# Keys in blocks of 64 throughout an attention stage: values on four tiles of the array

## The chip, the core and the metric

The kernel runs on one core of a Trainium2 chip. The core has a matrix engine (TensorE, PE in the profile, with PEld for its weight loads), a vector engine (VectorE, DVE), a scalar engine (ScalarE, ACT) and GpSimd (POOL); SyncE (SP) issues most of the transfers. Every engine works through its own instructions in order and waits for others by semaphores. PSUM, where TensorE writes its products, has eight banks of 512 fp32 columns on 128 partitions; all other on-chip data lie in SBUF. The metric is the device time of one execution in microseconds, as a median over runs.

## The reference

Attention with 8 batches, 8 heads, 576 positions and 64 channels a head. A query sees itself and the 127 positions before it, with a penalty that grows with the distance, by a slope for each head. The result goes, token by token, through a mixture of experts: a gate picks one of 8 experts for each of the 4608 tokens.

```python
rel = pos[:, None] - pos[None, :]
slopes = 2.0 ** (-8.0 * (np.arange(H, dtype=np.float32) + 1) / H)
bias = slopes[:, None, None] * (-np.abs(rel).astype(np.float32))[None, :, :]
mask = (rel >= 0) & (rel < window)                      # window = 128
scores = np.where(mask, scale * q @ k.T + bias, -1e9)
attn = np.exp(scores - max); attn = attn / (sum(attn) + 1e-9); x = attn @ v
logits = x @ w_gate; e = argmax(logits)                 # per token
y = gate_w * (relu(x @ w1[e]) @ w2[e])
```

## The kernel before

It has two stages. The first is attention, with the gate and the routing woven in; the second runs the experts over the rows that routing has sorted into DRAM. The change touches the first stage alone.

**Units.** Attention is cut into 32 units, one for each batch and pair of heads (`NU`, L497); a pair's 2 x 64 channels fill 128 partitions. The maximum isn't subtracted: exp(score) is multiplied by a table of exp(-slope x distance), which is zero outside the window. A unit goes through these steps:

- `scores` (L584): keys on the partitions, queries along the columns. Key blocks of 128 are taken as two halves of 64 keys (`HBLK`), each against the at most 192 queries that can see them, one product for each half and head, on a 64 x 64 quarter of the array. They fill four PSUM banks `sp`, 512 columns each; the corners that no product writes were cleared once (L520). ScalarE takes the exponential of each bank (L599).
- `factors` (L601): VectorE multiplies by the table, in two halves of the columns, 1024 elements each (L606, L611).
- `merge` (L613): VectorE adds two stretches of probabilities that belong to the same queries (L617), so that their sums need one product.
- `values` (L621): 128 keys by 64 channels as weights, the probabilities streamed, both heads beside each other on the columns of the array; queries 0 to 255 in one bank, 256 to 575 in another. ScalarE copies both to `xT` (L642).
- `totals` (L644): the sums of the probabilities for every query, by a product with a column of ones that selects a row for the pair of heads; all four pairs of a batch collect in one bank `sm`. At the batch's end `sm` is copied to `sT` (L669, L670).

**Tasks.** What follows attention for a batch is cut into tasks (`tasks_of`, L747): two for the gate's logits (`logits_t`), two or three `gate` tasks (transposes of logits and sums, L694 and L697, reciprocals, products with them, the minimum L713, then ScalarE's exponentials L716, and the pick of the expert), `row` (transposes of `xT` back to tokens and VectorE's scaling by 1/sum, L739), `place` (the rank of each token), and sends of rows by indirect transfers from POOL (L192).

**Order.** It is written out by hand (`manual_schedule`). In the main loop (L798 to L832) iteration u issues the loads for unit u + 4, scores of u, the first half of its factors, one task, the second half and the merge, then values and totals of unit u - 1, then two to four more tasks. Tasks start at u = 9. `last_tasks` (L768) handles the last batch, with the first layer of an early group of tokens put between.

**Buffers.** PSUM: four `sp` banks, one `sm`, and three `m` banks that values, logits, gate, place and row share in turn: each allocation waits until what stood in the bank three allocations before has been read. The load pool `ld` has five buffers each for queries and keys and two for values.

**Transfers.** SP issues queries, keys and values in the loop's order, with eight clearings of the routed rows between (`clear_rows`, units 1 to 10) and the first expert's weights at unit 16.

Of the kernel before, what the change touches and what calls it, by code (L numbers as in the profile page):

```python
# [8 lines left out]
F32 = mybir.dt.float32  # L9
I32 = mybir.dt.int32  # L10
# [5 lines left out]
P = 128  # L16
# [5 lines left out]
def kernel(  # L22
# [474 lines left out]
    NU = NB * HP  # L497

    BLK = [(j, 2 * P * j, P * j, 2 * P) for j in range(KT - 1)]
    BLK += [(KT - 1, 2 * P * (KT - 1), P * (KT - 1), P + HALF), (KT, 2 * P * KT - HALF, P * KT, HALF)]  # L500

    HBLK = []
    for j, c, q0, n in BLK[:-1]:
        HBLK += [(P * j, 0, c, q0, min(n, P + HALF)), (P * j + HALF, 1, c + HALF, q0 + HALF, min(n - HALF, P + HALF))]
    HBLK.append((P * KT, 1, BLK[-1][1], P * KT, HALF))
    W = 2 * P * KT
    SEG = ((0, 2 * P), (2 * P, S - 2 * P))
    QB = HP + 1
    with tc.tile_pool(name="tab", bufs=1) as tab, \
# [7 lines left out]

        sp_banks = [ps_s.tile([P, W // 2], F32, name=f"sp{i}") for i in range(4)]
        for sp in sp_banks:
            nc.vector.memset(sp[:], 0.0)  # L520

        rels = ex.tile([P, 2, W], F32, name="probs")
        rel_i, rel = rels.bitcast(I32)[:, 0, : 2 * P], rels[:, 1, : 2 * P]
        nc.gpsimd.iota(rel_i, pattern=[[1, 2 * P]], base=0, channel_multiplier=-1)
        nc.gpsimd.tensor_copy(rel, rel_i)

        fac2 = tab.tile([P, H, W // 2], F32, name="fac2")
        fac = fac2[:, :, : 2 * P]

        def distances(hp):  # L530
            pair = fac[:, 2 * hp : 2 * hp + 2, :]
            for i in range(2):
                nc.vector.tensor_scalar_mul(pair[:, i, :], rel, 2.0 ** (-8.0 * (2 * hp + i + 1) / H))
            nc.gpsimd.affine_select(
                pair, pair, compare_op=ALU.is_ge, fill=MASKED,
                base=0, pattern=[[0, 2], [1, 2 * P]], channel_multiplier=-1,
            )
            nc.gpsimd.affine_select(
                pair, pair, compare_op=ALU.is_gt, fill=MASKED,
                base=P, pattern=[[0, 2], [-1, 2 * P]], channel_multiplier=1,  # L540
            )

        def table(hp):
            heads = slice(2 * hp, 2 * hp + 2)
            nc.scalar.activation(fac[:, heads, :], fac[:, heads, :], AF.Exp, scale=-1.0)
            nc.vector.tensor_copy(fac2[:, heads, 2 * P : 3 * P + HALF], fac[:, heads, : P + HALF])
            nc.vector.tensor_copy(fac2[HALF:, heads, 3 * P + HALF :], fac[HALF:, heads, HALF:P])

        for hp in range(HP):
            distances(hp)  # L550
# [3 lines left out]
        nc.vector.memset(fac2[:HALF, :, 3 * P + HALF :], 0.0)  # L554
# [3 lines left out]
        for hp in range(HP):  # L558
            nc.vector.memset(one_c[:, hp, hp : hp + 1], 1.0)
# [8 lines left out]
        q_sb, k_sb, v_sb, xT, lT, sT = {}, {}, {}, {}, {}, {}  # L568
        early = {}
        probs, exps, mgs, sums = {}, {}, {}, {}  # L570
# [8 lines left out]
        def load_v(b):  # L579
            v_sb[b] = ld.tile([P, KT + 1, Dm], F32, name="v_sb", bufs=2)  # L580
            nc.sync.dma_start(v_sb[b][:, :KT, :], v[b * S : b * S + KT * P, :].rearrange("(t p) d -> p t d", p=P))
            nc.sync.dma_start(v_sb[b][:, KT, :], v[(b + 1) * S - P : (b + 1) * S, :])

        def scores(u):  # L584
            b, hp = divmod(u, HP)
            probs[u] = ex.tile([P, 2, W], F32, name="probs")
            sps = sp_banks[:2], sp_banks[2:]
            for k0, part, c, q0, n in HBLK:
                s, c = divmod(c, W // 2)
                for par in range(2):  # L590
                    half = slice(par * HALF, (par + 1) * HALF)
                    nc.tensor.matmul(  # L592
                        sps[s][par][part * HALF : (part + 1) * HALF, c : c + n], lhsT=k_sb[u][half, k0 : k0 + HALF],
                        rhs=q_sb[u][half, q0 : q0 + n], start=True, stop=True,
                    )
            exps[u] = [ex.tile([P, 2, W // 2], F32, name="e") for _ in range(2)]
            for s in range(2):
                for par in range(2):
                    nc.scalar.activation(exps[u][s][:, par, :], sps[s][par][:], AF.Exp, scale=D ** -0.5)  # L599

        def factors(u, s):  # L601
            hp, e = u % HP, exps[u][s]
            to = probs[u][:, :, s * (W // 2) : (s + 1) * (W // 2)]
            heads = slice(2 * hp, 2 * hp + 2)
            if s == 0:
                nc.vector.tensor_tensor(  # L606
                    to.rearrange("p a (j c) -> p a j c", c=2 * P), e.rearrange("p a (j c) -> p a j c", c=2 * P),
                    fac[:, heads, None, :].to_broadcast([P, 2, 2, 2 * P]), op=ALU.mult,
                )
            else:  # L610
                nc.vector.tensor_tensor(to, e[:], fac2[:, heads, :], op=ALU.mult)  # L611
# [581 lines left out]
```

## Time and profile before

| | |
|---|---|
| median of 3 runs (lowest, highest) | 727.13 us (725.44, 728.34) |
| the profiled execution, its time and span | 728.66 us, 726.9 us |
| busy: PE, PEld, DVE, ACT, POOL | 697.2, 562.7, 377.3, 225.3, 95.4 us |
| attention: first scores, scores of unit 9, scores of unit 31 | 5.09, 42.60, 187.90 us |
| DMA | 130.82 MB, mean 180 GB/s |
| L599 exponentials, 128x512, x128 | 66.8 us, mean 599 ns |
| L606 and L611 factors, 128x1024, x32 each | 39.2 and 39.0 us |
| L617 merge, 128x512, x32 | 22.1 us, mean 692 ns |
| L635 values on PE, x768 | 65.1 us |
| L642 copies of values, 256 and 320 columns, x32 each | 12.5 and 13.8 us |

Times are from the start of the span. The busy time of PE counts overlapping products once; an fp32 product appears as two instructions. A group of instructions is given by line, engine, operation, what it writes and reads, how often, its busy time and the mean of one. A bracket at the end of a line of the timeline is the time the engine stood idle before it, and who ended that.

### The profile page before, as it was taken

How to read it: one execution, taken by the hardware profiler on the slowest of the kernel's cores; microseconds unless marked ns; L12 is line 12 of the kernel's file. 1: busy time of each engine (PE TensorE's matmuls, PEld its weight loads, DVE VectorE, ACT ScalarE, POOL GpSimd, SP SyncE). 2: the span in 40 equal slices, each digit the busy share in tenths (PEclk: the TensorE clock that was granted, in tenths of full speed). 3: DMA queues.
4: the chain of work that ended last, by engine and by line, in shares of the span. 5: the costliest groups of instructions: out<-in, count | busy, mean ns of one | idle time of the engine just before them, and what ended most of it. 6: DMA issues, size and time to landing. Idle time of an engine off the chain costs nothing.

```text
span 726.9 us, 13073 instructions
## 1 busy us (share of the span) xinstructions
PE 697.2 (96%) x5414; PEld 562.7 (77%) x5414; DVE 377.3 (52%) x693; ACT 225.3 (31%) x538; POOL 95.4 (13%) x120
## 2 busy tenths in 40 slices
PE   7999999999999999999999999999999999999992
PEld 5877667667784768878897888888788878878881
DVE  9878678768762526246344634534363354326300
ACT  6765455455421212122121212212221312122130
POOL 5002322124321010020020002001100200110020
PEclk9999999999999999999999999999999999999997
DMA  9999896682213960285339037532913673173010
GB/s 327 365 372 375 227 395 169 190 230 75 89 73 120 344 217 24 108 302 165 132 114 334 29 130 257 214 131 77 330 69 131 208 261 123 55 264 110 1 59 7
DMA packets 54292, 130.82 MB, mean 180 GB/s; under 512 B 4175, under 2 KB 4175, under 8 KB 54224
## 3 DMA queue, kind: packets, MB, share of 16 engines
q1 hardware_dynamic: 47696, 110.97, 44.9%
q0 software_dynamic: 6000, 18.92, 7.0%
q8 instruction: 44, 0.72, 0.4%
q14 instruction: 24, 0.20, 0.1%
q10 hardware_dynamic: 528, 0.02, 0.0%
HBM read 102.55 MB, written 28.12 MB: 180 GB/s over the span
## 4 chain that ended last, share of the span: by engine, by line
PE 61%; issue 10%; POOL 1%; DVE 0%; ACT 0%; POOLq 0%; DVEq 0%
PE b L933 17%; PE a L933 11%; PE c L933 11%; PE a L479 6%; PE a L471 3%; PE b L471 3%; PE m L471 2%; PE sp L479 2%; PE c L471 2%; PE tp L462 1%; PE b L479 1%; POOL out_dram L430 1%; PE m L635 1%; PE m L736 0%; PE a L462 0%
## 5 line engine op out<-in xcount | busy, mean ns | idle before, releaser
L599 ACT ACTIVATE e<-sp 128x512 f32<-128x512 f32 x128 | 66.8, 599 | 35.6 <-PE sp L592 28.1
L430 POOL DMA_INDIRECT out_dram<-zo,si x28 | 29.5, 1052 | 326.1 <-ACT zo L1003 321.8
L635 PE MATMUL m<-probs,v_sb 128*64 128x256 f32 (+3 forms) x768 | 65.1, 314 | 3.2 <-DVE xs L739 2.2
L635 PEld LDWEIGHTS m<-probs,v_sb 128*64 128x64 f32 x768 | 48.3, 137 | 20.9 <-DVE xs L739 3.8
L592 PE MATMUL sp<-q_sb,k_sb 64*64 64x192 f32 (+2 forms) x1152 | 54.2, 323 | 6.0 <-DMA k_sb<-in_kT_dram 5.1
L592 PEld LDWEIGHTS sp<-q_sb,k_sb 64*64 64x64 f32 x1152 | 45.6, 138 | 16.9 <-issue 6.9
L192 POOL DMA_INDIRECT x_rows<-xs,slots x36 | 38.7, 1074 | 147.0 <-DMA k_sb<-in_kT_dram 48.0
L479 PE MATMUL a<-w,h 128*128 128x512 f32 x128 | 56.3, 592 | 0.0
L1003 ACT ACTIVATE zo<-zo,gw 128x256 f32<-128x256 f32 x42 | 19.1, 502 | 119.4 <-DVE zo L1014 78.2
L933 PE MATMUL a<-xgT,w 128*128 128x256 f32 x224 | 53.0, 379 | 0.0
L933 PE MATMUL b<-xTs,w1s 128*128 128x256 f32 x224 | 52.9, 379 | 0.0
L606 DVE TENSOR_TENSOR probs<-e,fac 128x1024 f32<-128x1024 f32 x32 | 39.2, 1225 | 25.2 <-ACT e L599 24.5
L933 PE MATMUL a<-w,h_sb 128*128 128x256 f32 x224 | 50.6, 379 | 0.0
L933 PE MATMUL b<-w2s,hs 128*128 128x256 f32 x224 | 50.6, 379 | 0.0
L933 PEld LDWEIGHTS a<-xgT,w 128*128 128x128 f32 x224 | 42.5, 190 | 8.7 <-issue 3.3
L933 PEld LDWEIGHTS b<-xTs,w1s 128*128 128x128 f32 x224 | 42.6, 190 | 5.8
L933 PEld LDWEIGHTS b<-w2s,hs 128*128 128x128 f32 x224 | 42.6, 190 | 5.8
L933 PEld LDWEIGHTS a<-w,h_sb 128*128 128x128 f32 x224 | 42.0, 190 | 5.4
L479 PEld LDWEIGHTS a<-w,h 128*128 128x128 f32 x128 | 23.7, 190 | 26.8 <-issue 26.8
L611 DVE TENSOR_TENSOR probs<-e,fac 128x1024 f32<-128x1024 f32 x32 | 39.0, 1219 | 3.1 <-ACT e L599 3.1
L963 DVE TENSOR_TENSOR u<-b,p 128x512 f32<-128x512 f32 x14 | 9.7, 692 | 56.1 <-PE b L933 56.1
L967 ACT ACTIVATE h_sb<-h_sb 128x512 f32<-128x512 f32 x14 | 8.8, 629 | 84.3 <-DVE h_sb L966 84.3
(210 smaller groups left out, 1163.3 us busy)
## 6 DMA issues: line engine op xcount, KB each, us to landing
w<-in_moe_w_dram SPq DMA_DIRECT2D x30, 2048.0 KB
q_sb<-in_qT_dram SPq DMA_DIRECT2D x32, 288.0 KB
k_sb<-in_kT_dram SPq DMA_DIRECT2D x32, 288.0 KB
x_rows<-zero_row SPq DMA_DIRECT2D x8, 1028.0 KB
xg<-x_rows SPq DMA_DIRECT2D x16, 514.0 KB
v_sb<-in_v_dram SPq DMA_DIRECT2D x8, 1024.0 KB
v_sb<-in_v_dram SPq DMA_DIRECT2D x8, 256.0 KB
xg<-x_rows SPq DMA_DIRECT2D x7, 257.0 KB
```

The source lines that it names most:

```text
L192: ins = nc.gpsimd.indirect_dma_start(out=x_d[:, :], out_offset=bass.IndirectOffsetOnAxis(ap=slots[:, t : t + 1], axis=0), in_=row, in_offs ...
L430: ins = nc.gpsimd.indirect_dma_start(out=out[:, :], out_offset=bass.IndirectOffsetOnAxis(ap=g["si"][:, j : j + 1], axis=0), in_=row, in_of ...
L471: nc.tensor.matmul(ps[:, :n], lhsT=g["w1"][:, db, fb * P : (fb + 1) * P], rhs=g["xT"][:, db, :n], start=(db == 0), stop=(db == DB - 1),)
L479: nc.tensor.matmul(ps[:], lhsT=g["h"][:, fb, j * P : (j + 1) * P], rhs=g["w2"][:, fb, :], start=(fb == 0), stop=(fb == FB - 1),)
L592: nc.tensor.matmul(sps[s][par][part * HALF : (part + 1) * HALF, c : c + n], lhsT=k_sb[u][half, k0 : k0 + HALF], rhs=q_sb[u][half, q0 : q0 ...
L599: nc.scalar.activation(exps[u][s][:, par, :], sps[s][par][:], AF.Exp, scale=D ** -0.5)
L606: nc.vector.tensor_tensor(to.rearrange("p a (j c) -> p a j c", c=2 * P), e.rearrange("p a (j c) -> p a j c", c=2 * P), fac[:, heads, None, ...
L611: nc.vector.tensor_tensor(to, e[:], fac2[:, heads, :], op=ALU.mult)
L635: nc.tensor.matmul(xp[par * HALF : (par + 1) * HALF, lo - q0 : hi - q0], lhsT=v_sb[b][:, j, h * D : (h + 1) * D], rhs=probs[u][:, par, c + ...
L933: nc.tensor.matmul(out_of[:, i, :], lhsT=lhs(i, k), rhs=rhs(k), start=(first and i == 0 and k == 0), stop=(k == nk - 1), skip_group_check= ...
L963: nc.vector.tensor_add(u2[:], bb, p1[:])
L1003: nc.scalar.activation(o[:, th, dh, i, :], src[:, i, :], AF.Copy, scale=g["gw"][:, j : j + 1])
```

## The change

All of attention takes keys in blocks of 64. The nine blocks of a batch are split into two groups, r = 0 with blocks 0 to 3 and r = 1 with blocks 4 to 8; group r lies on partitions 64r to 64r + 63. Each group has 768 columns for each head (W), so no column is left empty and a bank holds 384.

- Scores: the same 18 products a unit, in another order; four exponentials of 384 columns.
- Factors: two products, of 1152 and 384 elements, one after the other, and after `values` in the program.
- Values: 64 keys by 64 channels; the two groups and the two heads take the four quarters of the array. Each group has its bank. The groups overlap in 128 queries: ScalarE copies bank 0, VectorE copies 192 columns of bank 1 and adds its other 128 to `xT`.
- Totals: a column of ones for each half of the partitions gives both halves' sums in one product; eight products of 192 columns. `merge` goes. The rows are put together later by a new task `fold`, with three or four transposes, small reductions, adds and one reciprocal.
- Gate: three tiles a task in place of two; no transposes of sums.
- Order: values of u - 1 stand before the factors of u, all tasks at the end, three to five together, and a batch's tasks are added after them.
- The table is made by ScalarE alone, from one table of distances. Values are loaded into 64 partitions, 512 and 640 KB, where it was 1024 and 256 KB.

```diff
-        for k0, part, c, q0, n in HBLK:
-            s, c = divmod(c, W // 2)
-            for par in range(2):
-                ...
+        exps[u] = ex.tile([P, 2 * W], F32, name="e")
+        for first, last in ((0, 1), (1, 2), (2, 3), (3, None)):
             for par in range(2):
-                nc.scalar.activation(exps[u][s][:, par, :], sps[s][par][:], AF.Exp, scale=D ** -0.5)
+                head = slice(par * HALF, (par + 1) * HALF)
+                for r in range(2):
+                    for i, c, q0, n in BLK[r][first:last]:
+                        k0 = r * QB0 + i * HALF
+                        s, c = divmod(c, W // 2)
+                        nc.tensor.matmul(
+                            sp_banks[2 * par + s][r * HALF : (r + 1) * HALF, c : c + n],
+                            lhsT=k_sb[u][head, k0 : k0 + HALF], rhs=q_sb[u][head, q0 : q0 + n],
+                            start=True, stop=True,
+                        )
+        for s in range(4):
+            c = slice(W // 2 * s, W // 2 * (s + 1))
+            nc.scalar.activation(exps[u][:, c], sp_banks[s][:, : W // 2], AF.Exp, scale=D ** -0.5)
...
-    def merge(u):
-        ...
+    def values(u):
         ...
+        xp = [ps_m.tile([P, 4 * P], F32, name="m") for _ in range(2)]
+        for i in range(KT + 1):
+            for r in range(2):
+                for _, c, q0, n in BLK[r][i : i + 1]:
+                    keys = slice(r * HALF, (r + 1) * HALF)
+                    q0 -= r * QB0
+                    for par in range(2):
+                        h = 2 * hp + par
+                        nc.tensor.matmul(
+                            xp[r][par * HALF : (par + 1) * HALF, q0 : q0 + n],
+                            lhsT=v_sb[b][keys, i, h * D : (h + 1) * D], rhs=probs[u][keys, par, c : c + n],
+                            start=(i == 0), stop=(i == len(BLK[r]) - 1), skip_group_check=True,
+                        )
+        to = xT[pair][:, hp, o : o + S]
+        nc.scalar.copy(to[:, :QA], xp[0][:, :QA])
+        nc.vector.tensor_copy(to[:, QA:], xp[1][:, QA - QB0 : S - QB0])
+        nc.vector.tensor_add(to[:, QB0:QA], to[:, QB0:QA], xp[1][:, : QA - QB0])
...
+        for i in range(2):
+            for at in range(2):
+                for par in range(2):
+                    g = 32 * (2 * at + par)
+                    c = (2 * at + i) * C
+                    nc.tensor.matmul(
+                        sm[g : g + 32, i * HALF : i * HALF + C], lhsT=one_c[:, hp, :],
+                        rhs=probs[u][:, par, c : c + C], start=(hp == 0 and i == 0), stop=(hp == HP - 1),
+                        skip_group_check=True,
+                    )
...
+    def fold(b):
+        odd = b % 2
+        t0 = b // 2 * TP + odd * KT
+        m = ps_m.tile([P, 4, P], F32, name="m")
+        for i, n in enumerate([P, P, P] + [HALF] * odd):
+            nc.tensor.transpose(m[:n, i, :], s_rows[odd][:, i * P : i * P + n], ident[:])
+        def put(t, i, r, p0, n, first, src=None):
+            ...
+            if first:
+                nc.vector.reduce_sum(out, x, axis=AX)
+            else:
+                s2 = rows.tile([P, HP, 2], F32, name="s2")
+                nc.vector.reduce_sum(s2[p0 : p0 + n], x, axis=AX)
+                nc.vector.tensor_add(out, out, s2[p0 : p0 + n])
+        ...
+        nc.vector.reciprocal(rs, rs)
...
-            ts += [lambda i=i: gate(tiles, i) for i in range(0, len(tiles), 2)]
+            ts += [lambda: fold(b)] + [lambda i=i: gate(tiles, i) for i in range(0, len(tiles), LG)]
...
                 scores(u)
-                factors(u, 0)
-            do(0 if slow else 1)
+            if u > 0:
+                values(u - 1)
             if u < NU:
-                factors(u, 1)
-                merge(u)
+                factors(u)
                 ...
             if u > 0:
-                values(u - 1, 0)
-                values(u - 1, 1)
                 totals(u - 1)
-                if hp == 0 and u < NU:
-                    tasks += tasks_of(b - 1)
-            do(0 if slow else 2 if len(tasks) < 14 else 3 if len(tasks) < 20 else 4)
+            do(0 if slow else 3 if len(tasks) < 14 else 4 if len(tasks) < 20 else 5)
+            if u > 0 and hp == 0 and u < NU:
+                tasks += tasks_of(b - 1)
```

## The prediction

> **What bounds the kernel.** I read the busy slices first, then a table by stage, then TensorE's own sequence in a unit without other work, then the waits. Of the page's slices (40 equal parts of the span):
>
> ```profile
> PE   7999999999999999999999999999999999999992
> DVE  9878678768762526246344634534363354326300
> ACT  6765455455421212122121212212221312122130
> DMA  9999896682213960285339037532913673173010
> ```
>
> The table by stage (stretch, its length, busy time of each engine with instruction counts, granted clock, DMA share, GB/s):
>
> ```profile
> 5.00:42.00 37.00, 36.91 (x664) 29.93 (x668) 32.54 (x60) 26.77 (x58) 7.24 (x18) 1.00 1.05 373
> 84.00:188.00 104.00, 97.72 (x1505) 71.40 (x1505) 78.61 (x170) 57.39 (x159) 23.93 (x28) 1.00 0.65 205
> 232.00:727.00 495.00, 480.72 (x2374) 403.18 (x2372) 204.94 (x307) 106.46 (x228) 39.18 (x38) 0.99 0.44 155
> ```
>
> The experts (from 232 us) are 495 us of TensorE work that the change doesn't touch. What it can move lies before: TensorE works there nearly all the time, 36.91 of 37 us and 97.72 of 104, with VectorE at 88% and 76%. TensorE alone in units that have no routing tasks:
>
> ```profile
> 25.99 1.54 PE L592 MATMUL sp<-q_sb,k_sb 64*64 64x192 f32 x36
> 27.46 1.96 PE L635 MATMUL m<-probs,v_sb 128*64 128x256 f32 x24
> 29.35 0.62 PE L656 MATMUL sm<-probs,one_c 128*32 128x256 f32 x12
> ...
> 30.14 1.54 PE L592 MATMUL sp<-q_sb,k_sb 64*64 64x192 f32 x36
> ```
>
> Start to start: scores 1.47, values 1.89, sums 0.79; 4.15 us a unit. From unit 9 on (42.60) routing tasks come in; unit 31 starts at 187.90, so 22 units take 145.3 us, 6.6 each. The timeline of the gate of batch 5 shows what stops TensorE there:
>
> ```profile
> 158.03 1.54 PE L592 MATMUL sp<-q_sb,k_sb 64*64 64x192 f32 x36
> ...
> 159.98 0.20 DVE L713 TENSOR_REDUCE lmin<-lgn 128x5 f32<-128x40 f32 x1
> ...
> 160.21 0.30 ACT L716 ACTIVATE gex<-lgn,lmin 128x8 f32<-128x8 f32 x1 [3.52 <-DVE lmin L713]
> ...
> 161.64 2.02 ACT L599 ACTIVATE e<-sp 128x512 f32<-128x512 f32 x4
> ...
> 163.55 0.70 ACT L642 COPY xT<-m 128x256 f32<-128x256 f32 x2
> ...
> 163.97 0.66 PE L736 MATMUL m<-ident,xT 128*128 128x128 f32 x4 [1.14 <-ACT xT L642]
> ```
>
> ScalarE stands 3.52 us before the gate's exponentials, which wait for VectorE's minimum. Behind them queue the next scores' exponentials, behind those the copies that free two of the three m banks, and TensorE waits 1.14 us for a bank. The chain to watch is minimum, gate, exponentials, copy.
>
> [...] 36 score instructions of about 0.14 us pass in 1.47 us, nearly four at a time, and about 0.10 us passes at each change of mode (a last 64-column score product at 27.31, values at 27.46). [...] 692 ns for 512 elements and 1225 for 1024 are 1.04 ns an element.
>
> **TensorE's part.** A column of one pass takes 0.84 ns (experts: 379 ns rows start 0.216 us apart for 256 columns), and a product has two passes. Values now stream 2 heads x 1024 columns x 2 passes on two tiles: 1.72 us. The change makes it 2 x 1536 x 2 on four: 1.29 us, like the scores, which already have this count and these tiles. Scores and values share a mode, so one drain goes (0.10). Sums keep 768 columns a tile group (0.65) with 16 instructions for 20. New unit: 1.29 + 1.29 + 0.65, plus about 0.3 of drains and first weight loads: 3.5 us against 4.15. Over 32 units that is 20 us, if nothing else stops TensorE. Fold's three or four transposes (0.5 to 0.6, as the four of L736) replace those of the sums (0.26 a tile); even.
>
> **The other engines' part, a unit.** VectorE loses 1.22 + 1.22 + 0.69. It gains factors of 1152 and 384 elements (1.36 + 0.56 by the slope), a copy of 192 columns from PSUM (0.35, from 0.42 for 256) and an add of 128 (0.3): 2.57 for 3.13. Fold is 10 to 12 small operations a batch, at 0.17 to 0.2 each as the rows of L157 and L732: 2.1 us, less 0.7 of reciprocals. ScalarE's exponentials go from 2.06 to about 1.7, its copies from 0.82 to 0.49. Work falls everywhere, but the order in the queues gets worse in three places. The factors are no longer in two halves with a routing task between. The copies of unit u-1 stand before the factors of u on VectorE, and their add waits for ScalarE's copy, which stands behind the four exponentials of u. And all tasks stand after the factors, three to five together, where each holds one of the three m banks until VectorE reaches it.
>
> **Bare units.** From the start of scores: exponentials end at 2.85 (the last bank is ready at 1.5), ScalarE's copy 3.35, add 3.7, first factor 5.1; the next values need only that. With values 1.35 to 1.55 after their scores, a unit takes 3.6 to 3.75: nearly the whole saving, some 3 us by unit 9. But DMA is full here (1.05, 373 GB/s): the trace's semaphores put the values of batch 2 at 42.5 us, with 44.6 as their first use. The smaller value loads (1152 KB for 1280; three of them 0.39 MB, 1.05 us) bring that to 41.5. So I take **-2.5 us**.
>
> **Units with a gate.** Where fold and both gate tasks fall in one unit (program order: units 9, 12 and 30), I count from the scores of unit 12: factors end at 5.6; fold 7.7; five products with 1/sum (0.18 each) 8.6; reduction 0.74 and minimum 0.2: 9.6. TensorE, ahead, began the scores of 13 at 4.9. ScalarE: five gate exponentials (0.31 apart, fence above) 11.2, four exponentials 12.9, copy 13.4. VectorE: add 13.7, factors 15.6, first row 16.6. The second row's transposes wait for the copy, the fourth task (row 2) for the first row: unit 14 can begin at 17.2. Before, units 12 and 13 took 61.49 to 75.68, 14.2: +3.0. In the same way 9 and 10 give 16.5 for 13.8 and 30 and 31 give 13.9 for 11.8. Together **+7.8**.
>
> **The rest.** In units 15 to 28, where the gates are split over two units, the same count gives 5.2, 4.9, 7.4, 5.4 for a batch's four, 84.4 us in all, where the trace has 91.2 (84.43 to 175.68). Of those, about 3.7 are stops with no releaser on any engine (104.6 to 106.3, 128.4 to 130.5), which I expect again: **-3.1**. Units 11 and 14: 10.4 for 13.9, less 2 of such stops at 80 to 84: **-1.5**. Unit 29: **-1.3**. The end: two rows of batch 6 now come after unit 31 (+1.5), and the last fold's 2.1 us holds the banks that the last row and the early expert need (+1.7): **+3.2**. Two scatters of batch 6 move behind unit 31 on POOL, which stood idle 13.6 us before them, and the early gather on SP moves one unit later; it landed at 185.4 for a use at 197.3, so 12 us cover it. The post-routing chain and the last gathers keep their cover too: the early expert's second layer runs from 217.1 to 231.0, and the gathered rows land by 225.6; without it they would cost what is late beyond 5 us. At the start the tables' shorter chain is hidden by the first value load (10.4 us). Added DVE clearings (about 0.4 us) fall in bare units.
>
> Sum: -2.5 + 7.8 - 3.1 - 1.5 - 1.3 + 3.2 = +2.6 on the profiled execution (span 726.9, time 728.66), so 731.2 there. That execution lies 1.5 above the median of the runs, so **729.7**.
>
> **Bounds of the unknowns.** Values on four tiles with 64 keys aren't in the trace; the same shape for scores is. Cost: 1.29 at best, 2.6 if only two run at once; I take the first. The small reductions over a four-dimensional view: 0.17 to 0.3 each, at most +1 us a batch, of which a gate passes on all: 0 to +7; I take 0. The stops without releaser: -5 to 0 if they vanish; I take them as before.
>
> **Rivals.** *The saving gets through:* the bank waits overlap the gate's wait better than a count by hand shows. For it: TensorE's 94% busy share from 84 to 188; every engine has less work; TensorE's saving from unit 9 on is 23 x 0.65 = 15 us, and half of it beyond my sum gives 722. Against: the 3.52 us wait is there already. *The queue order costs more,* one mechanism: the add behind ScalarE's copy. It decides where the copy ends later than 3.7 after the scores. If each of the 23 later units lost 0.45 us more to it (one more task's turn in front), it is +10: 740. *The four tiles don't overlap* (the change doesn't do what it says): values 2.6 for 1.89, less the drain, +0.6 a unit on 727: 746. Against: the scores' 1.47. *TensorE's saving is hidden by DMA everywhere:* the DMA share of 0.65 after 84 us speaks against; it would give 727.
>
> **Chances.** My sum 0.50, from 723 to 735; the saving through 0.22; costlier order 0.20; no overlap 0.05; DMA 0.03. About 0.5%, 3.6 us, is what a measurement here tells from no change. Mine straddles the edge: 0.03 faster, 0.28 same, 0.19 slower. The saving through counts 0.20 faster and 0.02 same, the next two slower, DMA the same. So faster 0.23, same 0.33, slower 0.44. Range 719 to 741: it leaves out the best of the second case and the worst of the last two; my case's own is 723 to 735.
>
> **What would show it.** Scores to scores in units 3 to 8 near 3.7; values 1.3 after their scores; unit 9 starting near 39 to 40. ScalarE's wait for the minimum well above 19.6 us in all. In units 10, 13 and 31 TensorE waiting for m banks, 9 to 12 us long each. Wrong if those stay near 7, or if values take over 1.5.

## The result and the profile after

The changed kernel takes 755.32 us (median of 4 runs, 753.58 to 760.5) for 727.74 beside it: the ratio is 1.039, with a 95% interval from 1.034 to 1.045. It is slower by 28 us, and the forecast (729.7, range 719 to 741) is wrong. The profiled execution took 754.85 us, with a span of 753.1.

Of the page's slices, TensorE, its granted clock, the DMA share and the DMA rate:

```profile
PE   6888798888979999999999999999999999999992
PEclk9999999989989999999999999999999999999997
DMA  9999889964211494229236633913753481283010
GB/s 236 346 295 299 251 280 276 248 161 111 100 57 71 139 357 160 105 69 326 78 127 224 235 125 90 332 38 122 283 176 126 149 302 48 81 279 126 1 57 7
```

The DMA rate before, in the same slices:

```profile
GB/s 327 365 372 375 227 395 169 190 230 75 89 73 120 344 217 24 108 302 165 132 114 334 29 130 257 214 131 77 330 69 131 208 261 123 55 264 110 1 59 7
```

Before, TensorE had 9 in every slice but the first and last, and its clock 9 in all. Now TensorE is below 9 in ten of the first twelve slices, and the clock dips in slices 9 and 12. In slices 3 to 8 the DMA engines are busy for 80% or more and move 250 to 300 GB/s.

The table by stage: start of scores to unit 9, units 9 to 31, unit 31 to the second layer of the early expert (columns as before: stretch, length, busy time by engine, granted clock, DMA share, GB/s):

```profile
5.00:51.00 46.00, 38.41 (x740) 30.17 (x740) 23.48 (x60) 23.18 (x54) 0.43 (x2) 1.00 1.07 294
51.00:202.60 151.60, 132.47 (x2237) 101.61 (x2235) 98.08 (x298) 65.52 (x190) 32.73 (x42) 0.94 0.79 227
202.60:242.70 40.10, 33.94 (x282) 27.42 (x282) 23.73 (x91) 9.55 (x35) 9.61 (x13) 0.87 0.16 62
```

The same stretches took 37.6, 145.3 and 29.3 us before, with TensorE busy for 37.51, 136.50 and 28.42 of them. In the second TensorE is busy for 4 us less, but not in the first or the last, and in all three it now waits. The part of the change that was meant to save does save; a unit without a stop, on TensorE:

```profile
17.27 1.57 PE L592 MATMUL sp<-q_sb,k_sb 64*64 64x192 f32 x35
...
18.69 1.48 PE L625 MATMUL m<-probs,v_sb 64*64 64x192 f32 x34
20.10 0.86 PE L646 MATMUL sm<-probs,one_c 128*32 128x192 f32 x16
20.89 0.70 PE L592 MATMUL sp<-q_sb,k_sb 64*64 64x192 f32 x9
```

Values take some 1.5 us for 1.89, and scores follow scores after 3.62. Where such a chain stops, the profile shows three different things. First, TensorE's stops in the first nine units; "issue" means that nothing in the trace released it:

```profile
28.58 1.20 PE L625 MATMUL m<-probs,v_sb 64*64 64x192 f32 x25 [1.13 <-issue]
35.10 0.52 PE L646 MATMUL sm<-probs,one_c 128*32 128x192 f32 x3 [0.78 <-issue]
50.24 0.85 PE L646 MATMUL sm<-probs,one_c 128*32 128x192 f32 x13 [3.00 <-issue]
```

Second, the gate's queue, in unit 13:

```profile
83.97 0.20 DVE L737 TENSOR_REDUCE lmin<-lgn 128x5 f32<-128x40 f32 x1
...
84.20 0.30 ACT L740 ACTIVATE gex<-lgn,lmin 128x8 f32<-128x8 f32 x1 [5.00 <-DVE lmin L737]
...
87.24 0.51 ACT L632 COPY xT<-m 128x384 f32<-128x384 f32 x1
...
87.81 0.66 PE L760 MATMUL m<-ident,xT 128*128 128x128 f32 x4 [1.31 <-ACT xT L632]
...
90.73 0.66 PE L760 MATMUL m<-ident,xT 128*128 128x128 f32 x4 [1.90 <-DVE xs L763]
91.32 2.05 PE L592 MATMUL sp<-q_sb,k_sb 64*64 64x192 f32 x35
```

That is the predicted chain: minimum, gate exponentials, exponentials, copy, then a bank held by a row. The last line is the third thing: the same 36 scores that took 1.57 us take 2.05, since TensorE is granted half its clock from 92.2 to 95.6. There are six such stretches before 230 us, 27.3 us in all (from 51.3, 68.3, 92.2, 160.5, 211.7 and 225.3), each just after waits like the above; before there was none. Full clock is also first granted at 17.1 us, where it was 10.9; the table's 1.00 for the first stretch leaves out the time before.

### The profile page after: what moved, and what is told of

Read it like the earlier page. It is cut to its first block, busy times and chain, and to the rows that moved or that the text cites. A ratio compares the mean times of both kernels' runs of the same rounds, so it can differ in the third digit from the quotient of the medians.

```text
span 753.1 us, 13615 instructions
## 1 busy us (share of the span) xinstructions
PE 699.7 (93%) x5662; PEld 568.5 (75%) x5662; DVE 357.5 (47%) x782; ACT 207.9 (28%) x511; POOL 86.2 (11%) x114
## 4 chain that ended last, share of the span: by engine, by line
PE 59%; issue 10%; POOL 1%; DVE 1%; ACT 0%; POOLq 0%; DVEq 0%
PE b L954 17%; PE a L954 11%; PE c L954 11%; PE a L479 5%; PE a L471 3%; PE b L471 3%; PE m L471 2%; PE sp L479 2%; PE c L471 2%; PE tp L462 1%; PE b L479 1%; POOL out_dram L430 1%; PE m L625 0%; PE m L760 0%; PE a L462 0%
## 5 line engine op out<-in xcount | busy, mean ns | idle before, releaser
L625 PE MATMUL m<-probs,v_sb 64*64 64x192 f32 (+2 forms) x1152 | 63.9, 334 | 12.9 <-DVE xs L763 5.6
L625 PEld LDWEIGHTS m<-probs,v_sb 64*64 64x64 f32 x1152 | 56.4, 146 | 19.8 <-DVE xs L763 7.0
L599 ACT ACTIVATE e<-sp 128x384 f32<-128x384 f32 x128 | 55.0, 489 | 42.3 <-PE sp L592 33.7
L592 PE MATMUL sp<-q_sb,k_sb 64*64 64x192 f32 (+2 forms) x1152 | 58.3, 338 | 6.0 <-DMA k_sb<-in_kT_dram 5.1
L592 PEld LDWEIGHTS sp<-q_sb,k_sb 64*64 64x64 f32 x1152 | 48.9, 143 | 18.6 <-issue 11.4
L192 POOL DMA_INDIRECT x_rows<-xs,slots x36 | 36.3, 1008 | 179.1 <-DVE xs L756 72.6
L479 PE MATMUL a<-w,h 128*128 128x512 f32 x128 | 56.3, 592 | 0.0
L954 PEld LDWEIGHTS b<-xTs,w1s 128*128 128x128 f32 x224 | 42.6, 190 | 5.8
L954 PEld LDWEIGHTS b<-w2s,hs 128*128 128x128 f32 x224 | 42.6, 190 | 5.8
L605 DVE TENSOR_TENSOR probs<-e,fac 128x1152 f32<-128x1152 f32 x32 | 43.3, 1354 | 2.8 <-ACT e L599 2.8
L633 DVE COPY xT<-m 128x192 f32<-128x192 f32 x32 | 11.4, 355 | 62.7 <-PE m L625 48.3
L646 PE MATMUL sm<-probs,one_c 128*32 128x192 f32 x512 | 34.1, 350 | 5.4 <-issue 5.2
```

The source lines that it names most:

```text
L192: ins = nc.gpsimd.indirect_dma_start(out=x_d[:, :], out_offset=bass.IndirectOffsetOnAxis(ap=slots[:, t : t + 1], axis=0), in_=row, in_offs ...
L479: nc.tensor.matmul(ps[:], lhsT=g["h"][:, fb, j * P : (j + 1) * P], rhs=g["w2"][:, fb, :], start=(fb == 0), stop=(fb == FB - 1),)
L592: nc.tensor.matmul(sp_banks[2 * par + s][r * HALF : (r + 1) * HALF, c : c + n], lhsT=k_sb[u][head, k0 : k0 + HALF], rhs=q_sb[u][head, q0 : ...
L599: nc.scalar.activation(exps[u][:, c], sp_banks[s][:, : W // 2], AF.Exp, scale=D ** -0.5)
L605: nc.vector.tensor_tensor(to[:, :, : 3 * C].rearrange("p a (j c) -> p a j c", c=C), e[:, :, : 3 * C].rearrange("p a (j c) -> p a j c", c=C ...
L625: nc.tensor.matmul(xp[r][par * HALF : (par + 1) * HALF, q0 : q0 + n], lhsT=v_sb[b][keys, i, h * D : (h + 1) * D], rhs=probs[u][keys, par, ...
```

## The experiments

The kernel before takes about 727 us on some of the chips that the runs fell on and about 717 on the others. So a ratio is always to the kernel before on the same chip, and microseconds are set beside each other only within one group of chips, unless it is said. Most of what the chips differ by lies in units 9 to 31: the changed kernel takes 141.4 us there on one and 154.3 on another, and 550 after that on both.

| run | us | ratio to before (95%) | unit 9 at | units 9 to 31 | unit 31 to the end |
|---|---|---|---|---|---|
| *chips with 717* | | | | | |
| before, value loads in halves | 732.98 | 1.022 (1.021 to 1.024) | 45.4 | 146.9 | 538.5 |
| before, gate exponentials late | 714.15 | 0.996 (0.994 to 0.997) | 42.6 | 131.3 | 538.0 |
| changed kernel | 743.24 | 1.035 (1.033 to 1.037) | 51.3 | 141.4 | 550.0 |
| filler on TensorE | 739.05 | 1.032 (1.028 to 1.036) | 50.2 | 140.9 | 546.9 |
| gate exponentials late | 736.73 | 1.028 (1.026 to 1.030) | 52.0 | 135.8 | 546.1 |
| 128-partition loads | 733.33 | 1.021 (1.019 to 1.023) | 46.6 | 137.0 | 550.4 |
| 128-partition loads and filler | 727.96 | 1.014 (1.010 to 1.018) | 45.3 | 135.3 | 546.7 |
| 128-partition loads, old order, late clearings (2 runs) | 722.60 | 1.007 (1.005 to 1.009) | 44.5 | 132.1 | 545.4 |
| 128-partition loads, old order, late gate exponentials | 719.18 | 1.002 (1.001 to 1.003) | 44.7 | 129.7 | 545.5 |
| *chips with 727* | | | | | |
| before, once more | 725.06 | | 42.6 | 141.4 | 539.3 |
| before, new order | 726.89 | 0.999 (0.997 to 1.001) | 43.1 | 141.4 | 542.0 |
| changed kernel | 756.46 | 1.041 (1.039 to 1.043) | 52.4 | 154.3 | 549.6 |
| 128-partition loads, old order | 731.23 | 1.006 (1.005 to 1.008) | 44.5 | 141.3 | 544.0 |

The last three columns are from one profiled execution of each run, which can lie a few microseconds off the median.

**The loads, in the kernel before.**

```diff
-            nc.sync.dma_start(v_sb[b][:, :KT, :], v[...].rearrange("(t p) d -> p t d", p=P))
+            for r in range(2):
+                nc.sync.dma_start(v_sb[b][r * HALF : (r + 1) * HALF, :KT, :],
+                                  v[...].rearrange("(t r p) d -> r p t d", r=2, p=HALF)[r])
```

> The kernel before, with one edit: the 1024 KB load of a batch's values goes as two loads of 512 KB, one into partitions 0 to 63 and one into 64 to 127; bytes, order and everything else stay. Theory A (the half-width value loads of the changed kernel are what made its first nine units long): packets of these loads take about 150 ns where they took 84, the first values start near 13 us where they started at 10.6, unit 9 starts at 48 to 51 us for 42.6, and the time is 733 to 737 us. Rival B (the loads are harmless, the new order or the four tiles of values cost the start): unit 9 within 0.5 us of 42.6, time within 0.3% of before.

Measured: +15.5 us, twice what was expected, with not a byte or an instruction of the engines changed. A 2048-byte packet (most of those before 230 us carry values) took 145 ns at the median, for 84. The DMA rate by slices, and two of TensorE's waits up to 95 us:

```profile
GB/s 247 360 296 302 293 316 295 261 198 127 70 88 121 300 232 40 130 253 211 131 78 333 62 130 226 241 130 61 325 87 131 193 273 112 58 267 113 1 59 6
```

```profile
PE m L639 <- DVE xs L743: 6.1, 3, 5.4
PE m L639 <- DMA v_sb<-in_v_dram: 5.1, 2, 3.1
```

Unit 9 starts only 2.8 us late, at 45.4 and not at 48 to 51, and all of this lies before unit 2 (16.31 for 13.56); the rest comes after unit 9. The values of batch 2 are waited for 3.1 us, TensorE's clock is halved from 49.5 to 56.3, and TensorE waits 5.4 us for a bank in unit 14, because the row that holds it waits for a buffer that is still being sent from. Two loads, one for each half of the partitions, thus cost more than one load over all 128: 145 ns a packet against 84 and 336 GB/s against 379, at the same share of busy engines (1.06 and 1.05 from 10 to 42 us). So B falls, and theory A holds for the packets and the cost, though these loads alone don't make the first nine units as long as in the changed kernel.

**The loads, in the changed kernel.** The values lie in DRAM a second time (`vb`), in the order of the partitions; this copy is made on the host and isn't part of the time.

```diff
-            for r in range(2):
-                n, r0 = len(BLK[r]), b * S + r * QB0
-                nc.sync.dma_start(v_sb[b][r * HALF : (r + 1) * HALF, :n, :], v[r0 : r0 + n * HALF, :]...)
+            nc.sync.dma_start(v_sb[b][:, :4, :], vb[b * S : b * S + 4 * P, :].rearrange("(t p) d -> p t d", p=P))
+            nc.sync.dma_start(v_sb[b][HALF:, 4, :], vb[b * S + 4 * P : (b + 1) * S, :])
```

> The changed kernel, with the values laid out in DRAM once more in the order of its partitions, so that eight of a batch's nine blocks come by one load of 1024 KB into 128 partitions and the ninth by one of 128 KB into 64; the engines' instructions are the same. Theory A: unit 9 starts at 40 to 42 us for 51.0, the stop of 3 us at 47 and the half-clock stretch at 51.3 go, and the time is 743 to 747 us for 755.3. Rival B: unit 9 still starts after 48 us and the time stays within 0.5% of the changed kernel's.

Measured: 733.33 for 743.24, -9.9 us, in the middle of what was expected as a difference; packets back at 84 ns. But unit 9 started at 46.6, neither at 40 to 42 nor after 48: something else delays the start too. The stop of 3 us before unit 9 shrank to 1.35 but didn't go. The half clock at 51.3 went, and five stretches came after (59.4, 83.3, 107.2, 192.5, 206.2).

**The clock.**

```diff
+        def filler(n):
+            for _ in range(n):
+                last = at[0] >= NU - 1
+                nc.tensor.matmul(
+                    sp_banks[3][:, W // 2 :] if last else sums[max(sums)][:, 3 * P :],
+                    lhsT=ident[:], rhs=ident[:], start=last, stop=last, skip_group_check=True,
+                )
...
+                    if i == 0 and r == (u < NU - 1):
+                        filler(value_fill.get(u, 0))
...
             m = ps_m.tile([P, H, D], F32, name="m")
+            filler(row_fill.get(t, 0))
```

> The changed kernel, with 74 products of the identity by itself (128 columns, about 0.22 us each, into columns that nobody reads) put on TensorE just ahead of the instructions that stood waiting over 0.7 us for a PSUM bank, about as many as fill each wait. Order and waits of all else stay. Theory C (the waits cost a second time, because TensorE's clock is halved after them): the half-clock stretches at 68, 92, 160, 212 and 225 us go, 24 us of half clock in all, and the time is 744 to 750 us for 755.3. Rival D (where the clock is halved TensorE is not the bound, so it costs nothing): 754 to 757 us, the stretches gone all the same.

(There were 70 products, not 74.) This first run gave 739.08 us and a ratio of 1.032, where the changed kernel had 1.041 on another chip. Since the difference could be the chip's, both were run once more beside each other, with a third kernel that has the loads repaired as well.

> The changed kernel, unchanged, beside the two runs with filler. All theories: ratio to before 1.034 to 1.045 and six or seven stretches of half clock before 230 us, some 27 to 31 us in all.

> The changed kernel with the 70 filler products again, now on the same chip as the changed kernel itself. Theory C (the halved clock is a cost of its own): at least four of the stretches after 60 us gone, and the time 5 to 9 us (0.7 to 1.2%) below the changed kernel's. Rival D (it costs nothing, and the earlier difference in ratio came from the chip): within 0.3% of the changed kernel's.

> The changed kernel with both edits that leave the new order alone: 128-partition value loads and the filler products. Theory A and C (loads 2.0%, clock 0.9%, independent): ratio to before 1.008 to 1.014, no half-clock stretch between 60 and 230 us. If the two overlap (the late loads cause part of the half clock): 1.015 to 1.02.

Measured on one chip: 743.24, 739.05 and 727.96. Part of the first difference was indeed the chip's (the changed kernel has 1.035 there). The filler takes off 4.2 us, and 5.4 from the kernel with repaired loads. The executions of the first pair just overlap (741.3 to 744.5 and 737.9 to 743.7 us); that both pairs agree speaks for the gain, while its size is rough. Loads 9.9 and clock 4.2 make 14.1; both edits together took off 15.3. Within the noise they add up, with 1.014 at the upper end of what was expected, and one stretch of half clock (6.8 us from 120.9) where none was. The stretch from the last rows of batch 6 to the last gate, in the changed kernel and then in the one with filler beside it:

```profile
196.00:218.00 22.00, 16.68 (x164) 12.32 (x156) 14.50 (x55) 6.88 (x28) 4.32 (x6) 0.77 0.13 49
```

```profile
194.00:216.00 22.00, 20.43 (x220) 17.11 (x221) 15.09 (x56) 7.53 (x30) 4.30 (x6) 1.00 0.13 50
```

The filler holds the clock at 1.00 where it was 0.77. Half-clock time before 230 us goes from 30.7 us to 6.8. These 24 us could cost 12 if TensorE were the bound in all of them; they cost a third of that, so C holds in kind and was put somewhat too high (5 to 9 us). Rival D falls.

**ScalarE's queue.**

```diff
-            for t in ts:
-                gex = ...; nc.scalar.activation(gex[:], ..., bias=lmin[:, t : t + 1], ...)
+            waiting.append(ts)
...
+        def gate_exps():
+            for t in (waiting.pop() if waiting else ()):
+                gex = ...; nc.scalar.activation(gex[:], ..., bias=lmin[:, t : t + 1], ...)
...
             if i % RG == 0:
+                gate_exps()
...
                 values(u - 1)
+                gate_exps()
```

> The changed kernel, with ScalarE's gate exponentials held back until the next unit's exponentials and its copy of values are issued, so that these no longer queue behind the wait for the minimum. Theory E (the chain minimum, gate exponentials, exponentials, copy makes the long unit pairs): ScalarE's wait of up to 5 us before the gate exponentials goes, units 9 and 10 take 13 to 14.5 us for 16.7, units 12 and 13 13 to 14 for 16.6, the half-clock stretches at 68, 92 and 212 us go, and the time is 742 to 748 us. Rival F (VectorE's fold and the bank held by each task make them, whatever ScalarE's order): the pairs stay within 0.7 us and the time within 0.4% of the changed kernel's.

Measured: 736.73, 6.5 us under the changed kernel on a chip of the same speed. Units 9 and 10 take 14.9 us (16.5 in the changed kernel there), 12 and 13 take 14.9 (17.1), and the end 3.9 less; all this falls just short of E's figures. The wait goes in units 10 and 13 and after the last unit. In units 17 to 31 ScalarE still waits five times for a minimum, up to 5.1 us. In unit 13 the copy now stands ahead of the wait:

```profile
83.95 0.48 ACT L632 COPY xT<-m 128x384 f32<-128x384 f32 x1 [1.85 <-PE m L625]
84.33 0.30 ACT L746 ACTIVATE gex<-lgn,lmin 128x8 f32<-128x8 f32 x1
...
84.94 1.09 PE L766 MATMUL m<-ident,xT 128*128 128x128 f32 x8
...
88.21 0.65 PE L766 MATMUL m<-ident,xT 128*128 128x128 f32 x4 [1.81 <-DVE xs L769]
```

The row behind the copy no longer waits; the wait of 1.8 us for a bank that VectorE's row holds is as long as before. Of the pairs' excess over the kernel before (2.8 and 3.2 us, with that kernel's pairs taken from the other group of chips) 1.1 and 1.0 are left. So E holds for about two thirds of it; that fold and the held banks make the rest, as rival F says, was not tried. Three stretches of half clock remain after the start, at 52.7, 151.6 and 206.3 us.

**The order.** The same two kernels were run with the loop's order exchanged: the old order in the changed kernel with repaired loads, the new order in the kernel before.

```diff
-            if u > 0:
-                values(u - 1)
+            do(0 if slow else 1)
             if u < NU:
                 factors(u)
...
             if u > 0:
+                values(u - 1)
                 totals(u - 1)
-            do(0 if slow else 3 if len(tasks) < 14 else 4 if len(tasks) < 20 else 5)
-            if u > 0 and hp == 0 and u < NU:
-                tasks += tasks_of(b - 1)
+                if hp == 0 and u < NU:
+                    tasks += tasks_of(b - 1)
+            do(0 if slow else 2 if len(tasks) < 14 else 3 if len(tasks) < 20 else 4)
```

> The kernel before, unchanged, for a profile on the same chip as the runs beside it. All theories: starts of units and stretches at half clock as in its first profile, within 2 us up to unit 31; what differs in the stage of the experts is the chip's.

> The changed kernel, unchanged, on the same chip as the runs beside it: the yardstick for the edits of it. All theories: its ratio to before as first measured, 1.034 to 1.045, with six stretches of half clock before 230 us.

> The kernel before with one edit: the new order of the main loop (values of u-1 ahead of the factors of u, all tasks at the end, three to five together, a batch's tasks added after them); blocks of 128 keys, loads, merge and gate as they were. Theory I (the order alone makes the long unit pairs and the long end): the units of the gates of batches 2 and 7 and the end grow by 2 to 4 us each, half-clock stretches come after them, and the ratio is 1.011 to 1.025. Rival J (the order costs only together with fold and the add): within 0.5% of before.

> The changed kernel with two edits: values loaded into 128 partitions from the second layout, and the old order of the main loop (factors of u ahead of the values of u-1, one task between the scores and the factors, two to four at the end, a batch's tasks added before those). Theory G (loads and order hold the whole loss, the four tiles of values do save): unit 9 starts at 40 to 42 us, units 9 to 31 take 130 to 140 us, from unit 31 to the end it takes 539 to 543 us, and the ratio to before is 0.98 to 1.0. Rival H (fold, or the add of the two banks, costs wherever it stands): units 9 to 31 take over 143 us, and the ratio is 1.0 to 1.02.

The kernel before with the new order is at 0.999: theory I falls. Its pairs 9 and 10, and 12 and 13, grew by 0.9 and 1.0 us and its end by 2.6, as the theory says but less, and two stretches of half clock came (78.3 and 112.4); units 15 to 28 gave 3.2 back (87.8 for 91.0). In the changed kernel the old order, with the loads, takes off 25 us (1.041 to 1.006), where the loads alone took off 9.9 on the other chips; on those the old order, together with a later place for some clearings (below), takes off 10.7 more (733.33 to 722.60). So the order costs mainly together with the rest of the change, as rival J says. That it is fold and the add of the two banks, because these lengthen VectorE's part between two copies, is argued from the gate's queue above, not tried alone. Theory G falls: unit 9 at 44.5, units 9 to 31 in 141.3, the end in 544.0 and the ratio of 1.006 all lie above its figures. Rival H has its point: 1.006 isn't 1.0, units 9 to 31 are no shorter than before (if not over its 143 us), and the end is 4.7 us longer.

**TensorE's own stops.** In this last kernel TensorE stops four times with no releaser before unit 9, 3.5 us in all:

```profile
24.07 1.20 PE L622 MATMUL m<-probs,v_sb 64*64 64x192 f32 x24 [0.76 <-issue]
30.29 0.35 PE L643 MATMUL sm<-probs,one_c 128*32 128x192 f32 x1 [0.63 <-issue]
36.75 1.53 PE L622 MATMUL m<-probs,v_sb 64*64 64x192 f32 x34 [0.73 <-issue]
43.74 0.84 PE L643 MATMUL sm<-probs,one_c 128*32 128x192 f32 x11 [1.40 <-issue]
```

Counted from the start, 705, 961, 1217 and 1473 of TensorE's instructions stand ahead of them (products, weight loads, and the few by which it only waits): 256 apart, whatever the work is. In the changed kernel the stops shown above stand at 705, 961 and 1473, and a wait of 0.5 us that the profile puts down to VectorE at 1217. The page's DMA queues have one for instructions, with packets of 16 KB (47 of them, 0.77 MB, in the changed kernel), and a packet of it begins 2.4 to 2.7 us ahead of the end of each stop. To test this, the eight clearings of the routed rows (1028 KB each) were moved to units 7 to 10.

> The changed kernel with the 128-partition value loads and the old order of the loop, with one edit more: the eight clearings of the routed rows, spread over units 1 to 10, all go in units 7 to 10, so that the transfer engines have gaps in units 3 to 6. In the run without this edit TensorE stopped with no releaser after 706, 963, 1219 and 1474 of its instructions (0.76, 0.63, 0.73, 1.40 us). Theory K (TensorE's instructions come by the same full transfer engines, 256 at a time, and it has used them up): the stops at 706, 963 and 1219 shrink below 0.3 us and unit 7 starts at 32 to 33 us for 34.2; the load moves to units 8 to 12 and costs there, so the time itself may go either way by 1%. Rival L (the stops belong to the work, or fetching is that slow by itself): stops of 0.6 us and more at the same counts.

```profile
23.48 1.20 PE L622 MATMUL m<-probs,v_sb 64*64 64x192 f32 x24 [0.52 <-issue]
34.75 1.53 PE L622 MATMUL m<-probs,v_sb 64*64 64x192 f32 x34 [0.29 <-issue]
43.12 1.49 PE L643 MATMUL sm<-probs,one_c 128*32 128x192 f32 x11 [2.77 <-issue]
```

The stops at 961 and 1217 (963 and 1219 in the text above) are gone or under 0.3 us, the one at 705 is 0.52, above what was expected, and unit 7 starts at 32.6 for 34.2. Where the clearings now go, the stop at 1473 has grown to 2.77. The stops follow the transfers and not the work: K holds, and L falls. The kernel before has no stop of this kind before unit 9. It uses 160 products and weight loads in 4.15 us, which is 256 in 6.6; the changed kernel uses 176 in 3.6, which is 256 in 5.2. In the changed kernel, packets of instructions begin 6.4 to 7.3 us apart from 18.9 to 39.1 us, in the kernel before 6.3 to 7.0 from 15.5 to 41.9: often enough for a kernel that needs one every 6.6 us, not for one that needs one every 5.2.

**All repairs, and the best of the kernel before.**

> The changed kernel with all three repairs: 128-partition value loads, the old order of the loop, and ScalarE's gate exponentials held back until the next unit's exponentials and copies are issued. Theory M (what is left of the loss after loads and order is half ScalarE's queue): units 9 to 31 take 135 to 138 us for 141.3, the ratio to before is 0.996 to 1.002. Rival N (what is left is the stops of TensorE in the first nine units and the longer end, which ScalarE's queue does not touch): ratio 1.003 to 1.008.

> The kernel before with one edit: ScalarE's gate exponentials held back until the next unit's exponentials and copies are issued. Theory M: TensorE's waits of 1.1 to 1.3 us for ScalarE's copies in the units of batches 3 and 5 and some smaller ones go, ratio 0.993 to 0.998. Rival (these waits are passed on to VectorE's rows, which need the exponentials' sums): within 0.2% of before.

With all three repairs (loads, order, gate exponentials) the changed kernel is at 1.002 (1.001 to 1.003), at the upper edge of M's range and just slower than before; units 9 to 31 take 129.7 us, 2.4 less than in the kernel with late clearings on a chip of the same speed. The same late gate exponentials in the kernel before give 0.996 (0.994 to 0.997): TensorE's waits of 1.1 to 1.3 us for ScalarE's copies are gone. This is the fastest of all, faster than both kernels, if by 0.4%. Between these two, on one chip: unit 9 is 2.0 us later in the repaired kernel, units 9 to 31 take 1.6 less, and the end 7.5 more. In units 9 to 31 its values take 7.0 us less of TensorE (35.4 for 42.4, start to start), its transposes of logits and sums 2.2 less, its scores 2.8 more and its waits 4.6 more.

## Why the prediction was wrong

| step of the prediction | predicted, us | measured, us |
|---|---|---|
| start to unit 9 | -2.5 | +8.4 |
| units 9 and 10 | +2.7 | +3.0 |
| units 12 and 13 | +3.0 | +2.4 |
| units 30 and 31 | +2.1 | +2.7 |
| units 11 and 14 | -1.5 | +0.6 |
| units 15 to 28 | -3.1 | +1.7 |
| unit 29 | -1.3 | +0.3 |
| from the values of unit 31 to the end | +3.2 | +7.2 |
| sum | +2.6 | +26.3 (span: +26.2) |

**What held.** Values on four tiles take 1.5 us, at the bound that the text gave for being wrong but well under the 2.6 of tiles that don't overlap; scores follow scores after 3.6 to 3.8 where nothing stops. The 0.10 us between scores and values, the prediction's drain, is gone: the first product of the values starts at 18.62 us, the last of the scores at 18.64. The three gate pairs, counted by hand through the queues, are right to 0.3 to 0.6 us each; units 10 and 13, and 31 up to its values, are 9.5, 11.9 and 10.0 us long, and ScalarE's wait for the minimum rose as forecast: 30.5 us in 8 waits for 19.6 in 7. Some of this closeness is luck: on the other chip with 727, units 12 and 13 take 18.9 us, 5.0 more than before.

**"The smaller value loads ... bring that to 41.5": the step that failed most.** It priced a load by its bytes and left out that it goes to 64 partitions, although the description of the change said so. The values of batch 2 came at 48.9 and 52.0 us, not at 41.5. Undoing this one thing is worth 9.9 us, 1.3% of the time; doing it alone costs 15.5. No rival had it. It shows in the first six DMA slices: busy as before, at 70 to 120 GB/s less in four of them. But the values of batch 2 aren't what TensorE stood for: it took them up at 53.4 without a wait. The start is late in two other places. Unit 2 starts at 17.27 us for 13.54, after a wait of 1.4 us for the values of batch 0 and with full clock first granted at 17.1; the text had taken the first load of values to be as before. And the stop before unit 9 is long. On the chips with 717, loads into 128 partitions bring unit 2 from 17.07 to 14.42 us and this stop from 3.54 to 1.35, which makes the 4.7 us by which unit 9 comes earlier.

**"Bare units" counted TensorE's products but not what brings its instructions.** The changed kernel has a tenth more of them a unit, in less time. Stops with no releaser cost it 4.9 us by unit 9, where 3 us of saving were counted.

**TensorE's saving was mis-sized.** A unit was put at 3.5 us for 4.15; where nothing stops it takes 3.62. Scores stay at 1.5 and sums at 0.79; only the values pay, some 0.4 us a unit in the bare units and 0.3 later (7.0 us over 22). 20 us over 32 units should have read about 12. The step for units 15 to 28 is also summed wrongly: 5.2, 4.9, 7.4 and 5.4 us for a batch's four units give at most 81.5 us for fourteen, not 84.4. With that sum the step would have been further off.

**The clock was taken as granted.** The sums for units 11 and 14, for 15 to 28 and for the end use durations of a trace at full clock. The filler runs put the halved clock at 4 to 5 us in all. At the end it is plain: the values of unit 31 take 3.42 us and their sums 1.51 (2.2 and 0.86 in the kernel with all repairs, which has full clock there), and the first layer's 24 products 7.11 for 5.37 before; 3.6 us of the 4.0 by which that step was wrong. The waits ahead of it can be short: two gaps of 1.3 and 1.9 us with 1.0 us of work between (from 86.5 us) were enough for the half clock from 92.2. In the profile of the changed kernel all 14 changes of the clock lie whole multiples of 3.413 us apart. If its time is cut at these points, TensorE was busy for 1.0 to 1.6 us of the 3.4 ahead of each of the six stretches. A wait of 1.8 us at 112.1 that falls across such a point, with 2.8 and 2.3 us of work on its two sides, was not followed by half clock. A bank wait thus can be paid for twice (filler alone gave 4.2 us back), and the sum of waits priced it once.

**The rivals.** Costlier queue order (740) was nearest in kind; it had the sign right, but put the price on the add behind ScalarE's copy in every unit. The runs give 6.5 us to the gate exponentials in ScalarE's queue, and 14 to these and the order together (733.33 to 719.18, on chips of one speed). How much of that is the clock kept up, and how much the queues themselves, they don't separate. The end of the repaired kernels stays open. With loads and old order it is 4.7 us longer than before at full clock, and 3.1 of these lie between the values of unit 31 and the first layer of the early group. With all three repairs it is 7.5 us longer than in the kernel before with late gate exponentials; a wait of 1.6 us behind the last fold and 6.8 us at half clock are part of that. What the rest consists of was not tried.

## What to carry to other kernels

Price a load by the partitions that it reaches (here 145 to 158 ns a packet for 84), and look at the GB/s row beside the DMA share: here a full share at a lower rate (1.07 and 309 GB/s from 5 to 42 us, where it was 1.05 and 373) was a worse load, not more data. Price a wait on TensorE in work that is due in the next few microseconds too, since the clock can fall after it (0.77 of full speed in one stretch of 22 us). And where transfers are saturated, count instructions as well as columns: smaller tiles needed more of them here (176 a unit for 160), their packets are among the transfers, and TensorE stood up to 3.0 us at a time.

## What the runs showed of the hardware

- Loads into 64 partitions: 158 ns for a 2048-byte packet at the median before 230 us in the changed kernel and 145 in the kernel before with halved loads, against 84 with loads into 128, at the same busy share of the DMA engines (1.05 to 1.07).
- Before unit 9, TensorE's stops of over 0.6 us with no releaser stood 256 of its instructions apart, or twice that, and in the changed kernel each ended 2.4 to 2.7 us after the start of a 16 KB packet of the instruction queue. There, with a DMA share of 1.07, these packets began 6.4 to 7.3 us apart, its units use 256 instructions in 5.2 us, and it stopped for 0.8 to 3.0 us at three such points. With the clearings moved out of units 3 to 6, two of the stops shrank from 0.63 and 0.73 us to under 0.3.
- Half clock came in stretches of 3.4 or 6.8 us in the changed kernel, on a grid of 3.413 us. In its profile and that of the kernel before, from the first full clock to 700 us, the six intervals of this grid at full clock in which TensorE was busy for 1.03 to 1.61 us were followed by half clock, and none of the 387 in which it was busy for 1.69 us or more. Identity products that nobody reads raised the clock from 0.77 to 1.00 in the stretch above.
